# Loads of the later batches: each released by a score unit of its own, none by a program block; a new order of TensorE's units

## The chip, the cores and the metric

The kernel runs on one core of one Trainium2 chip. The metric is the time of one execution on the device in microseconds (us). The kernel before takes 405.16 us, the median of three runs (404.38 to 405.39).

## The reference

Inputs are q, k and v (8 batches, 12 heads, 448 positions, head size 64) and three weight matrices, all in float32. The kernel computes with bf16 operands, sums in f32 and writes f32.

```python
scores = q @ k.T / sqrt(64)                   # for each batch and head, 448 x 448
attn   = maximum(scores, 0) ** 2 / 448
x      = (attn @ v), heads side by side       # 3584 tokens x 768
g, val = x @ w_gate, x @ w_val                # 768 -> 1536 each
out    = (gelu(g) * val) @ w_out              # 1536 -> 768, f32, 3584 x 768
```

## The kernel before, in words

**Tiling.** A batch is 448 tokens. TensorE works as four quarters of 64 rows by 64 columns: nearly every matmul instruction is a 64x64 tile, the two column quarters of a row half get their matmuls one behind the other, and the two row halves (called 0 and 1) run beside each other, each with its own stream of work. The code keeps two lists for them, PE0 and PE1; a *unit* is a run of operations on row half 0 and, behind or beside it, the matching run on row half 1.

There are these kinds of unit:
- *score unit* (`add_scores`): 64 keys against 448 queries for two heads, or, for the last key block of a pair, for four heads with half the work each. There are 21 per batch, seven per group of four heads. A group of four heads of a batch is called a *third* here. Behind a score unit ScalarE does the ReLU (`emit_relu`, L695, out of PSUM tile `sp` into `rl`) and VectorE squares two units at a time (L709, `rl` into `attnT`).
- *value unit* (`add_values`): attention times v for two heads; the result goes to `xT`.
- *gate and value units* (`add_gate_value`) and *pair units* (`add_pair`): the two up-projections. The pair units do two 128-column blocks in seven half-size products, with sums of tokens (`ts`) and of weights (`ws`) made by VectorE ahead.
- *product units* (`add_product`): the down-projection, again as seven half-size products, with sums of `uT` (tiles `s`) and of the weights (`wt`). ScalarE copies some results into `osb` (L1205), VectorE adds the others (L1203), and SP stores finished tiles (L1221).

**What sets the order.** The string `LINE` gives the order of the gate, pair and product units: a single digit is a gate or value unit of that batch, `6A7` is product 7 of pair unit A of batch 6, `m4` is product 4 of token group m. The string `SHIFT` moves, for batches 2 to 7, the start and the end of the stretch over which a batch's score and value units are spread between them. A planner (`run_plan`) then takes units and operations one by one, keeps clocks for the engines and PSUM banks from costs written in the code, and so settles the order in which each engine's instructions are written into the program. On the chip each engine runs its own list in that order, and semaphores hold an instruction until what it needs is there.

**How a late third comes in.** Batches 0 and 1 are loaded up front and transposed on TensorE. The 18 thirds of batches 2 to 7 each take six loads on the POOL queue: q in two column parts, k in two column parts (`load_qk`, L407, 128 KB and 96 KB) and v in two halves (`load_v`, L426, 128 KB). When q and k are there, VectorE regroups them into `qkr` (L458), and SP issues two DMA transposes into `qkT` (L463). The score units then read `qkT`.

**What releases a late load.** Two things, both in the code around L1405 to L1418. First, `op.behind`: a load may not be issued before the ReLU of one named score unit of an earlier third has run (three thirds back for q and k, two for v). `PACE` says which of the seven units: `0, 0` for the two parts of q, `1, 2` for k, `4, 5` for v. Second, `op.gate`: the planner keeps a list of *marks*. TensorE's program comes in blocks of 256 instructions, and `Blocks` notes the matmul at which the next block is expected to be asked for. A load with a gate is put behind the latest mark (a semaphore on that matmul, added in `load`'s `paced`), and only if the loads since that mark fit into `BLOCK` = 7.1 us of the planner's time. The transposes on SP have such a gate too (`GATE_T` = 1.2).

```python
GATE_T, BLOCK = 1.2, 7.1
...
if not forced and max(traffic, t + 1.3) + op.gate > at + span:
    return None
```

Of the kernel before, what the change touches and what calls it, by code (L numbers as in the profile page):

```python
# [9 lines left out]


LINE = """
0 0 0 0 0 0 0 0 0 0 0 0 0 0 0 0 0 0 0 0 0 0 0 0 a1 1A1 1 1 1 2 a7 1 a2 1 1 1A6 1A2 1 a6 1 2 2A1 a5 1
1 2 1 1 1 2 1A7 2 1 a4 1 1A4 1A5 1 1 1A3 1 1 1 b1 b6 b7 a3 c1 c7 b5 2 b4 c6 2 2A7 2 2A6 2A5 b3 c5 2
c3 2A2 b2 2 2B1 2 2 c4 2B6 2A4 2B2 2B7 2B4 2A3 2B5 2 2 2 2 2B3 d1 3B1 d2 3B2 3B6 d7 3 3B7 3A1 c2 3A7
3 e1 3 3C1 3A6 d6 d5 3A2 3 3 3 3A5 3B4 e6 3A4 3C6 e7 3 3A3 d4 3C7 d3 e5 3B5 3 3C2 3 3C5 3B3 3 4C1
3C4 3C3 e2 3 3 4A1 4A2 4C6 e3 4C2 f1 f6 4A6 4 e4 4A7 f7 f2 f4 4C7 4D1 4B1 4 4C4 4B7 4 4B6 4 4D2 4A5
4B2 4B5 4 4 4C5 4D6 g1 4D7 g6 g7 4A4 4D5 g2 g4 5B1 5C1 4D4 4B4 4C3 5 f5 4 5B2 4A3 5C2 4B3 5 f3 4D3
5B6 5C6 g5 5C7 4 5A1 5C4 5B7 5 h1 5 5A6 5C5 h6 5A7 5D1 5 5A2 h2 h7 5 5B4 g3 5B5 5C3 5A5 5B3 5A4 6A1
5D7 5D2 h5 5D6 5D5 5D4 5 5A3 5D3 6A2 5 h3 i1 6B1 h4 6A7 i7 i2 6B2 6C1 i6 6B7 6C2 i5 6C6 6C7 j1 6D1  # L20
i4 6A6 6D6 6E1 6D7 j7 6A4 6F7 6D2 6A5 6E2 6B6 6A3 6D4 6E7 6F1 6B5 6F2 i3 6B4 6F6 6F5 6E6 6E5 6C5 6F4
j6 6E4 6C4 6F3 6C3 7E1 j2 6E3 6B3 7A1 7E2 6D5 7A2 j4 6D3 k1 7A7 k7 7E7 k2 k6 7E6 7B1 7C1 7B2 7B7 k5
l1 l7 7C7 7C2 7C6 j5 7D1 7A6 7E5 j3 l6 k4 7D6 7F1 7E4 7D2 7C5 7B6 7B4 7E3 7F6 7C4 l5 7A5 7F7 l2 7D7
7A4 7B5 7C3 7F5 k3 7F2 7B3 7D5 7D4 l3 7A3 7F4 7D3 7F3 m7 m1 l4 n1 m6 n7 n6 m5 n5 m3 n4 n3 m4 m2 n2
"""


# [3 lines left out]
"""  # L31


SHIFT = "-285.5 -165 37.25 3 -152 -99.5 -4.75 -19.75 18.25 -42.25 -369.75 2"


class Op:
# [223 lines left out]
def kernel(  # L261
# [30 lines left out]
    OGS = d_model // NG  # L292
    WOG = 3
    SB = 2
    PACE = 0, 0, 1, 2, 4, 5
    FB = 4
    FILL = 30.0
    EARLY = 2
# [60 lines left out]
    arrivals = {}  # L359
# [947 lines left out]
    for b in range(B):  # L1307
# [8 lines left out]
        if b >= EARLY:  # L1316
            lo, hi = lo + float(SHIFT.split()[2 * (b - 2)]), hi + float(SHIFT.split()[2 * (b - 2) + 1])
        if b >= EARLY:
# [89 lines left out]
    for n, (b, m) in enumerate(thirds):  # L1408
        if (b, m) > (2, 1):
            for i, op in enumerate(qk_loads[b, m]):  # L1410
                op.behind.append(relus[(*thirds[n - 3], PACE[i])])
        if (b, m) >= (2, 0):
            for i, op in enumerate(v_loads[b, m]):
                op.behind.append(relus[(*thirds[n - 2], PACE[4 + i])])
        for op in (*qk_loads[b, m], *v_loads[b, m]):
            op.deps += op.behind
            if b >= EARLY:
                op.gate = arrivals[op]  # L1418
    for new, old in zip(duos[RING_A:], duos):
        gone = [o_op[b, pr] for keys in old["of"] for b, pr, _ in keys]  # L1420
        for sq in new["sq"]:
# [46 lines left out]
```

## Time and profile before

| what | value |
|---|---|
| median of three runs | 405.16 us (404.38 to 405.39) |
| the profiled execution | 403.54 us, of it the span 401.5 us and 2.0 us around it |
| TensorE clock granted | 0.997 of full speed, mean |
| busy: TensorE matmul, weight load | 97%, 88% of the span |
| busy: VectorE, ScalarE, POOL | 77%, 65%, 24% |
| DMA bytes by POOL queue (q0) and by SP queue (q1) | 24.39 MB, 19.08 MB |

How to read it: busy times are shares of the span. A matmul's record has a modelled end, so TensorE can be counted busy while it waits; distances from one matmul's start to the next one's are exact, and the text uses those. A 64x64 matmul over 448 columns holds its quarter for 0.189 us (from start to start of matmuls on one quarter), over 224 columns for 0.096 us.

### The profile page before, as it was taken

To read this page: it belongs to the slowest core of one execution; us is meant where nothing else is said; L and a number is where in the kernel's file an instruction comes from. 1 tells how busy PE (TensorE), PEld (TensorE's weight loads), DVE (VectorE), ACT (ScalarE), POOL (GpSimd) and SP (SyncE) were. 2 spreads that over 40 slices of the span, in tenths; PEclk is the share of its full clock that TensorE was granted. 3 is DMA by queue.
4 is the path that set the end of the run, shared out by engine and by line. 5 is a ranking of instruction groups with operands and counts; after the bars stand their busy time and mean duration, and the time that the engine had idled before them with its cause. 6 is when DMAs were issued, how large, how long until landed. Compare 5 with 4: busy or idle time off the path is not lost.

```text
span 401.5 us, 22878 instructions
## 1 busy us (share of the span) xinstructions
PE 389.7 (97%) x10570; PEld 352.3 (88%) x10573; DVE 310.0 (77%) x522; ACT 259.6 (65%) x401; POOL 96.7 (24%) x156
## 2 busy tenths in 40 slices
PE   7999999999999999999999999999999999999994
PEld 3456788889997889988999999999999999999993
DVE  2785779877888679988898788568899988866671
ACT  4865772357686668868776787747787875525430
POOL 7567304423233233133331332103110000000000
PEclk9999999999999999999999999999999999999998
DMA  8999997998999987999499986736871301111115
GB/s 108 179 198 198 197 209 105 152 129 134 151 102 208 107 98 98 113 174 137 62 154 138 126 135 87 94 82 76 76 137 22 81 6 45 42 45 43 44 42 157
DMA packets 85086, 45.11 MB, mean 112 GB/s; under 512 B 45952, under 2 KB 81536, under 8 KB 84992
## 3 DMA queue, kind: packets, MB, share of 16 engines
q0 software_dynamic: 46944, 24.39, 49.6%
q1 hardware_dynamic: 37888, 19.08, 26.3%
q8 instruction: 82, 1.34, 1.4%
q10 hardware_dynamic: 160, 0.20, 0.2%
q14 instruction: 12, 0.10, 0.1%
HBM read 48.76 MB, written 11.01 MB: 149 GB/s over the span
## 4 chain that ended last, share of the span: by engine, by line
PE 97%; issue 1%; ACT 0%; DVE 0%
PE ff L349 84%; PE sp L349 9%; PE ff L548 1%; PE ff L1399 1%; PE sp L627 1%; PE ff L627 1%; PE ff L590 0%; ACT rl L695 0%; ACT qkT L598 0%; ACT osb L1205 0%; DVE warm L334 0%; DVE table L337 0%
## 5 line engine op out<-in xcount | busy, mean ns | idle before, releaser
L695 ACT ACTIVATE rl<-sp 128x896 bf16<-128x896 f32 x168 | 152.1, 919 | 55.2 <-PE sp L349 48.3
L349 PE MATMUL ff<-xT,wg 64*64 64x224 bf16 (+1 forms) x2304 | 180.5, 299 | 0.0
L349 PEld LDWEIGHTS <-wv 64*64 64x64 bf16 x2304 | 120.7, 107 | 8.2 <-issue 2.6
L349 PEld LDWEIGHTS <-wg 64*64 64x64 bf16 x2304 | 121.5, 107 | 6.1
L349 PE MATMUL ff<-xT,wv 64*64 64x448 bf16 x1056 | 120.6, 349 | 1.1 <-issue 0.9
L709 DVE TENSOR_TENSOR attnT<-rl 128x1792 bf16<-128x1792 bf16 (+1 forms) x98 | 92.3, 952 | 11.6 <-ACT rl L695 11.2
L349 PEld LDWEIGHTS <-ws 64*64 64x64 bf16 x1872 | 92.9, 107 | 1.9 <-issue 1.3
L349 PEld LDWEIGHTS <-s 64*64 64x64 bf16 x1344 | 82.5, 107 | 2.6
L349 PE MATMUL ff<-attnT,v 64*64 64x448 bf16 (+1 forms) x768 | 82.1, 326 | 0.3 <-issue 0.2
L349 PE MATMUL ff<-ts,ws 64*64 64x224 bf16 x1248 | 77.9, 256 | 1.4 <-issue 1.4
L349 PE MATMUL sp<-qkT 64*64 64x448 bf16 (+1 forms) x768 | 77.2, 331 | 1.5 <-issue 0.9
L349 PE MATMUL ff<-ts,wv 64*64 64x224 bf16 x1248 | 78.0, 256 | 0.0
L349 PE MATMUL ff<-wo,uT 64*64 64x384 bf16 x672 | 65.8, 322 | 0.0
L349 PEld LDWEIGHTS <-uT 64*64 64x64 bf16 x1008 | 63.1, 107 | 2.3 <-issue 0.9
L349 PE MATMUL ff<-wo,s 64*64 64x384 bf16 x672 | 64.4, 323 | 0.0
L947 DVE TENSOR_TENSOR part<-ff,part 128x448 f32<-128x448 f32 x78 | 47.4, 622 | 20.1 <-PE ff L349 13.9
L349 PE MATMUL ff<-wt,s 64*64 64x384 bf16 x672 | 62.7, 323 | 0.0
L426 POOL DMA_DIRECT2D v<-in_v_dram x48 | 29.6, 621 | 97.3 <-ACT rl L695 37.9
L943 ACT COPY part<-ff 128x448 f32<-128x448 f32 x78 | 41.2, 534 | 14.6 <-PE ff L349 12.8
L349 PEld LDWEIGHTS <-v 64*64 64x64 bf16 x768 | 45.6, 107 | 4.2 <-issue 1.8
L407 POOL DMA_DIRECT2D qk<-in_q_dram x43 | 27.2, 636 | 79.7 <-ACT rl L695 40.9
L349 PEld LDWEIGHTS <-qkT 64*64 64x64 bf16 x768 | 37.8, 106 | 8.3 <-issue 5.7
(51 smaller groups left out, 418.2 us busy)
## 6 DMA issues: line engine op xcount, KB each, us to landing
out_dram<-osb SPq DMA_DIRECT2D x54, 192.0 KB, 3.5
v<-in_v_dram POOLq DMA_DIRECT2D x48, 128.0 KB, 4.4
wg<-in_moe_w_gate_dram POOLq DMA_DIRECT2D x6, 384.0 KB, 10.1
wv<-in_moe_w_val_dram POOLq DMA_DIRECT2D x6, 384.0 KB, 11.2
wo<-in_moe_w_out_dram POOLq DMA_DIRECT2D x4, 576.0 KB, 15.4
qk<-in_q_dram POOLq DMA_DIRECT2D x18, 128.0 KB, 3.5
qk<-in_k_dram POOLq DMA_DIRECT2D x18, 128.0 KB, 4.9
qk<-in_q_dram POOLq DMA_DIRECT2D x18, 96.0 KB, 4.6
```

What stands on the lines that cost most here:

```text
L349: ins = nc.tensor.matmul(o, lhsT, rhs, start=start, stop=stop, skip_group_check=onto, tile_position=(P * row, P * col))
L407: return nc.gpsimd.dma_start(qk16[b, m][HALF[i], r0:r0 + h1 - h0, cols], src[b, h0:h1].rearrange("h (p c) d -> p h (c d)", c=SC)[:, :, cols])
L426: return nc.gpsimd.dma_start(v16[b, m][HALF[i], h0 % 4:h0 % 4 + h1 - h0, :, :], v[b, h0:h1].rearrange("h (p c) d -> p h c d", c=SC)[:, :, ...
L548: blocks.add(nc.tensor.matmul(t[:, :], warm[:, 0:128], warm[:, :], start=True, stop=True))
L627: blocks.add(nc.tensor.transpose(t[HALF[j], c, :], src[:, 2 * r + j, c, :], ident[:, :], tile_position=(0, P * j)))
L695: relu.ins = nc.scalar.activation(duo["rl"][:, u % 2, :, :], box[0][:, :, 0:S], AF.Relu).ins
L709: nc.vector.tensor_tensor(a[:, part], duo["rl"][:, part], duo["rl"][:, part], op=ALU.mult)
L943: rd.ins = nc.scalar.copy(st["t", name][:, :], box[0][:, 0:S]).ins
L947: rd.ins = nc.vector.tensor_tensor(t[:, :], box[0][:, 0:S], t[:, :], op=ALU.add).ins
L1399: blocks.add(nc.tensor.matmul(t[HALF[j], :], warm[:, HALF[j]], warm[:, :], start=True, stop=True, tile_position=(0, P * j)))
```

## The change

Three things change. `PACE` becomes `0, 1, 2, 3, 4, 5`, so the six loads of a third wait for six different score units. The late loads lose `op.gate`: they no longer wait for a mark, and the planner no longer counts whether they fit behind it; the transposes on SP keep theirs. `LINE` and `SHIFT` are written anew, which changes the order of the units; the program is the same for the first 1,650 of TensorE's 21,181 instructions (the first 52 us of the trace). The set of matmuls is the same (10,573).

```diff
 LINE = """
-0 0 0 0 0 0 0 0 0 0 0 0 0 0 0 0 0 0 0 0 0 0 0 0 a1 1A1 1 1 1 2 a7 1 a2 1 1 1A6 1A2 1 a6 1 2 2A1 a5 1
...
-7A4 7B5 7C3 7F5 k3 7F2 7B3 7D5 7D4 l3 7A3 7F4 7D3 7F3 m7 m1 l4 n1 m6 n7 n6 m5 n5 m3 n4 n3 m4 m2 n2
+0 0 0 0 0 0 0 0 0 0 0 0 0 0 0 0 0 0 0 0 0 0 0 0 1 1A1 1 2 1A6 2 2 1 1A7 1A2 1A5 2 a1 2 a2 2A1 1A4 1
...
+7F4 7D6 7D5 7D4 7D3 l2 7F5 7A4 7C5 7C3 7E3 7A3 l5 l4 7F3 m1 n1 m7 k3 l3 m2 m6 n6 m5 n7 n4 m3 n5 n2
+m4 n3
 """
...
-SHIFT = "-285.5 -165 37.25 3 -152 -99.5 -4.75 -19.75 18.25 -42.25 -369.75 2"
+SHIFT = "-183 -79.5 40.75 1.75 -343.75 -112 43.75 -179.5 27.25 -513.5 -447.25 0.25"
...
-    PACE = 0, 0, 1, 2, 4, 5
+    PACE = 0, 1, 2, 3, 4, 5
...
         for op in (*qk_loads[b, m], *v_loads[b, m]):
             op.deps += op.behind
-            if b >= EARLY:
-                op.gate = arrivals[op]
```

More of the change, by code (lines that the diff above doesn't have):

```diff
@@ L12 @@
 LINE = """
-0 0 0 0 0 0 0 0 0 0 0 0 0 0 0 0 0 0 0 0 0 0 0 0 a1 1A1 1 1 1 2 a7 1 a2 1 1 1A6 1A2 1 a6 1 2 2A1 a5 1
[L14 to L22, printed above, removed]
@@ L23 @@
-l1 l7 7C7 7C2 7C6 j5 7D1 7A6 7E5 j3 l6 k4 7D6 7F1 7E4 7D2 7C5 7B6 7B4 7E3 7F6 7C4 l5 7A5 7F7 l2 7D7
-7A4 7B5 7C3 7F5 k3 7F2 7B3 7D5 7D4 l3 7A3 7F4 7D3 7F3 m7 m1 l4 n1 m6 n7 n6 m5 n5 m3 n4 n3 m4 m2 n2
+0 0 0 0 0 0 0 0 0 0 0 0 0 0 0 0 0 0 0 0 0 0 0 0 1 1A1 1 2 1A6 2 2 1 1A7 1A2 1A5 2 a1 2 a2 2A1 1A4 1
+1 1 1A3 1 2 1 2A2 a6 1 2A7 a7 2 1 a5 1 1 2A6 2 2 1 1 1 1 a3 1 1 a4 1 1 b1 b7 c1 b2 b6 2A4 2 c6 b4 b5
+c7 c5 2B1 2B6 c4 2B2 c3 b3 2A5 2 c2 2B7 2B4 2B5 2A3 2 3A1 2 3A2 2 2B3 2 2 3A6 3A7 d7 d1 3B1 d2 4C1
@@ new lines @@
+3B2 3 3C1 3B7 3 d6 3 e1 d4 3C7 3 3C6 3 3B6 e7 3B4 e6 3A4 3A5 3 3 3 3C2 3 3B5 3 3 d5 3C4 3A3 3C5 d3
+4A1 4C2 3B3 3C3 e5 3 4A7 f1 f2 f6 e4 f7 4C7 4 e2 4C6 4A2 e3 g7 4B1 f5 4B6 4 4A6 4B2 g1 4B7 4 g2 4A5
+4C5 4A4 4B4 4B5 f4 4D7 4D1 4C4 4 5B1 5 4D6 4D5 4A3 4 g6 4 g5 4C3 4B3 f3 4 5 5B2 4D2 4D4 g3 4D3 5C1
+g4 5B6 5B7 5C2 5B5 5A1 4 5A6 5 5C7 5A7 5A2 5 5B4 5D1 h1 5A4 5D6 5D2 h6 5C6 h7 5 5D7 5D5 5A5 6A1 5B3
+5 5C5 5C4 5A3 5C3 5D4 6B1 5 5D3 5 6A2 6B2 h4 i1 i2 6B7 6A6 i7 h5 6A7 h2 6D1 6F7 6D7 h3 j1 6D6 6C1
@@ L25 @@
+6D2 i6 j7 6E1 j6 6C7 6C2 6E7 i5 i4 6C6 6B6 6A5 6A4 6E6 6A3 6F1 6B4 6B5 6C5 6D5 6D4 6F6 i3 6B3 6F5
+6C4 j5 6D3 6E2 6F2 6E5 6F4 6C3 6F3 6E4 6E3 7E7 j2 7E1 7B1 k1 k7 7E2 7A1 7B2 7B7 k2 7B6 7E6 j4 7C1 k6
+7A2 l7 7C7 7C6 7A7 7B4 7C2 l1 7B5 7B3 k5 7A6 7F1 j3 7D1 7E5 7F7 7F2 7A5 k4 7F6 7E4 l6 7D7 7C4 7D2
+7F4 7D6 7D5 7D4 7D3 l2 7F5 7A4 7C5 7C3 7E3 7A3 l5 l4 7F3 m1 n1 m7 k3 l3 m2 m6 n6 m5 n7 n4 m3 n5 n2
+m4 n3
 """
```

## The prediction, made before the changed kernel was run

> **What bounds the kernel now.** I read the page's busy times first, then the chain, then the waits of TensorE, and last the stretches of 40 us.
>
> ```profile
> span 401.5 us, 22878 instructions
> PE 389.7 (97%) x10570; PEld 352.3 (88%) x10573; DVE 310.0 (77%) x522; ACT 259.6 (65%) x401; POOL 96.7 (24%) x156
> ...
> q0 software_dynamic: 46944, 24.39, 49.6%
> q1 hardware_dynamic: 37888, 19.08, 26.3%
> q8 instruction: 82, 1.34, 1.4%
> ...
> PE 97%; issue 1%; ACT 0%; DVE 0%
> ```
>
> TensorE is the bound: the chain is its own work for 97%. The row q8 is its program being fetched by DMA: 82 packets for 10570 + 10573 instructions, so one packet of 16 KB per 256 instructions.
>
> ```profile
> 120.00:160.00 40.00, 38.19 (x979) 34.72 (x974) 31.66 (x50) 28.79 (x42) 12.49 (x20) 1.00 0.97 127
> 160.00:200.00 40.00, 38.90 (x1089) 36.54 (x1084) 34.05 (x56) 29.97 (x46) 11.48 (x19) 1.00 0.91 122
> 240.00:280.00 40.00, 40.00 (x1233) 39.39 (x1227) 29.20 (x49) 26.08 (x44) 6.73 (x11) 1.00 0.59 83
> ```
>
> The columns are length, then busy TensorE, weight load, VectorE, ScalarE, POOL, granted clock, DMA share and GB/s. TensorE has holes where the DMA share is above 0.9 and none where it is 0.59, at the same clock of 1.00. The waits of TensorE say what kind of hole it is:
>
> ```profile
> PE ff L349 <- issue: 2.5, 5, 0.9
> PE sp L349 <- issue: 0.9, 1, 0.9
> ```
>
> These are all of TensorE's waits between 100 and 330 us, and all are "issue": no semaphore is late. One of them up close, with the loads that POOL issued before it:
>
> ```profile
> 140.00 0.38 PE L349 MATMUL ff<-xT,wg 64*64 64x448 bf16 x2
> 141.33 0.28 PE L349 MATMUL ff<-ts,ws 64*64 64x224 bf16 x2 [0.95 <-issue]
> ```
>
> ```profile
> 134.75 1.22 POOL L407 DMA_DIRECT2D qk<-in_q_dram  x2 [5.31 <-ACT gel L1025]
> 135.96 0.63 POOL L407 DMA_DIRECT2D qk<-in_k_dram  x1
> 136.76 0.62 POOL L407 DMA_DIRECT2D qk<-in_k_dram  x1 [0.17 <-PE ff L349]
> ```
>
> In the trace's packets of q8 the fetch for this place starts at 138.51, takes 1.17 us, and TensorE goes on 1.65 us behind its end. The other holes look the same. From start to start, less the normal step, TensorE stands still at 128.7 (1.1 us), 140.0 (1.2), 177.0 (1.0), 187.0 (0.5), 192.4 (0.4), 215.7 (0.7) and around 317 to 322 (0.7), in sum 5.7 us with 0.1 of scatter; each ends 1.2 to 1.65 us after a q8 packet has landed. When a fetch meets little traffic, its packet starts before TensorE is 35 instructions into the next block; before these seven it is 77 to 131 instructions in. So the seven holes are fetches that stood behind other DMAs, and they are the stall time that a change of load timing can touch. Before five of the seven (128.7, 140.0, 177.0, 192.4 and 215.7, in sum 4.4 us) the four q and k loads of one third had been issued within 2.0 to 3.8 us, as in the rows above; before the hole at 187.0 stand v loads, a transpose and stores, before the last one stores alone.
>
> **The change part by part.** The profiled execution is 403.54 us: span 401.5 and 2.0 around it. The median is 1.6 above it. I work the sum as a difference on the profiled one and put it on the median, 405.16.
>
> *The new order on TensorE, taken by itself.* The matmuls are the same. I walked both lists with the steps that the trace shows (0.189 us per 448 columns, 0.096 per 224, each row half by itself). The old order walked so follows the trace to 0.1 us between the seven holes, so it can carry a difference. Where one row half has nothing next in the list while the other works, time is lost: 0.7 us in the old order behind 45 us, 1.6 us in the new one (the largest are 0.2 to 0.4 us on one half, eight of them, around 72, 162, 250 to 262 and 299 us). Cost: +0.9 us. It is on the path, since nothing covers TensorE.
>
> *The release of the loads.* 108 late loads, issued between 65 and 299 us, so one per 2.2 us in the mean; 28 of the 107 distances are under 0.8 us, which is POOL working through a bunch (one issue is 0.62 us). With six different units per third, and POOL's program no longer holding a load for a mark, the q and k loads of a third come about one score unit apart, some 2.2 us each, so the four take some 6.5 us where the bunches took 2.0 to 3.8. This thins the traffic ahead of a fetch. Against it: nothing now keeps a load from arriving just ahead of one. The trace does not show late loads without marks. Its bounds: the least is that all seven holes go, −5.7 us. The most, from the nearest rows: the up-front weight loads have no marks either, and fetches under them start 3.5 to 4.4 us behind the point where an undisturbed one starts 0.6 to 1.7 us behind it; were five more of the late fetches hit as the seven are (0.8 us each), it would be +4.1 us. I take a value between: of the 4.4 us that follow bunches of four loads half stays (2.2), and the two others stay (1.2). Left 3.4 instead of 5.7 us: −2.3 us. I choose the lower half because the bunch stands before five of seven holes and the bytes do not change; new holes are a rival below.
>
> *Waits for data.* A q or k load now hangs on a unit up to one place later, 2.2 us. Behind it stand the regrouping (L458), two transposes on SP's queue, and the third's first score. In the trace the second transpose lands 1.4 us ahead of the first score at 82.8, 4.6 at 95.4, 1.8 at 108.1 and 7.7 us or more ahead for all fifteen thirds after that. The last q or k load is issued 15.7 us ahead of the first score at the first late third and 25.9 us or more at the others. So I cost the later load at nothing; the cover is this lead. In the three early thirds the transposes, which keep their marks, decide, not the loads; with 1.4 to 1.8 us of cover a transpose that comes one block mark later (3 to 6 us) would cost 1.5 to 4 us. POOL's queue holds nothing but loads, so nobody else waits behind a held load; on SP's queue stores (L1221) stand behind a held transpose, and the four `osb` buffers hold back ScalarE's copies, for which the trace shows no wait by TensorE.
>
> *The end.* The last products are m4 and n3 instead of m2 and n2. The last read is a ScalarE copy (L1205, 479 ns in the mean) in place of a VectorE add (L1203, 556 ns), and the same four stores follow. I take 0; it may be 0.1 us either way.
>
> Sum: +0.9 − 2.3 + 0 + 0 = −1.4 us, so 402.1 on the profiled execution's own time and 403.8 on the median.
>
> One rule of the Trainium skill speaks against this reading. "Runtime: NRT & Kernel Launch", in the section on instruction fetch mechanics, says that a program is streamed in 16 KiB blocks of 256 instructions and that crossing a block is mostly hidden. The trace agrees with the block (82 packets) and not with the hiding (5.7 us in seven places). By that rule the fifth rival would hold. A second, from "DMA: Bandwidth & Descriptors", section "Queues, rings and completion order", says that a DMA engine goes round its queues packet by packet, so that a fetch would wait for one packet per queue and not for whole loads. The trace shows waits of 3 to 5 us behind sustained traffic where single data packets last 0.03 to 0.18 us, so I do not count on it.
>
> **The rivals.**
> - *More fetches are hit (slower).* Without marks a load arrives ahead of a fetch by chance, at any of the 50 fetches between 65 and 300 us, with a DMA share over 0.9 up to 240 us. For: the early unmarked loads delay every fetch under them. Against: they are 384 KB each and back to back. It decides from the point where the holes' sum passes 4.8 us (5.7 − 0.9); at nine holes of 0.8 us, 7.6 us, the time is 405.16 + 0.9 + 1.9 = 408.0.
> - *As many holes as now, in other places (no change).* Sum 4 to 6 us: 404.4 to 406.4, all inside 0.3% of the median; at 5.0 us, 405.4. For: traffic and fetches are as many, and the transposes and stores are still there. Against: the bunches go.
> - *Nearly all holes go (faster by more).* Only the two without a bunch of four stay, 1.2, or less: 405.16 + 0.9 − 4.5 = 401.6, and 401.1 with the store hole alone. For: the bunches are what five of seven have in common. Against: a transpose and a store or two also make up the traffic.
> - *A third's transposes come late (slower).* The early thirds have 1.4 to 1.8 us of cover; two of them late by one mark beyond that, 2 us each, give 403.8 + 4 = 407.8.
> - *The holes have nothing to do with the loads (no change).* Then they stay, at 5.7 us in sum, and the order alone counts: 405.16 + 0.9 = 406.1. For: the hole at 317 to 322 us has no load near it. Against: from 240 to 280 us, at a DMA share of 0.59, there is no hole at the same rate of instructions. The page on the runtime, named above, would give this time too.
>
> **How the numbers follow.** 0.3% of 405 is 1.2 us; that is about what a measurement of this kernel can tell from no change. Chances: the forecast's own case (holes of 2.5 to 4 us) 0.33, nearly all gone 0.12, as many as now 0.22, not the loads 0.05, more hit 0.21, late transposes 0.07. The first case reaches from 402.8 to 404.3, and 404.0 is the bound of 0.3%, so some 0.06 of it falls inside; of "more hit" nothing falls inside by its definition, and 0.04 of "as many" goes over to slower for scatter. That gives faster 0.33 − 0.06 + 0.12 = 0.39, same 0.06 + 0.18 + 0.05 = 0.29, slower 0.21 + 0.07 + 0.04 = 0.32. The range: below it reaches to 400.8, the store hole alone with 0.3 of scatter; above to 408.4, nine holes with 0.4. The forecast's own range is 402.6 to 404.6.
>
> **What the changed profile would show.** The holes are again "issue" waits of TensorE and each ends some 1.5 us behind a q8 packet; there are four or five, in sum some 3.4 us. POOL's waits for late loads name the ReLU (L695 before, one line on after) and no longer matmuls, and fewer than ten distances are under 0.8 us. The walk of the new order leaves 0.9 us more. I am wrong if TensorE waits for a semaphore of VectorE or of a transpose, or if the holes' sum is over 5 us.

## The result and the profile after

| kernel | median | lowest to highest | executions |
|---|---|---|---|
| before | 405.39 us | 402.29 to 412.97 | 19 |
| after | 402.40 us | 400.90 to 404.77 | 19 |

The ratio of after to before is 0.9926, with a 95% interval of 0.9907 to 0.9945: the change makes the kernel about 3.0 us (0.7%) faster. The forecast was 403.8, so the direction was right and the gain twice what I had worked out (−3.0 in place of −1.4). 402.40 lies inside the whole range (400.8 to 408.4) and just below the forecast's own (402.6 to 404.6). Ratios here leave out executions that lie more than 1.5% above the fastest of the same kernel, which trims a kernel whose time scatters widely, so medians of all executions stand beside them.

The profiled execution of after took 402.81 us (span 400.7), that of before 403.54 (span 401.5). Their difference is only 0.7, and this is the first thing to learn from: the profiled execution of before lies 1.9 us under the median of before in the table, that of after 0.4 above its own. Lines of the page of after:

```profile
span 400.7 us, 22892 instructions
PE 391.1 (98%) x10573; PEld 357.8 (89%) x10573; DVE 309.4 (77%) x522; ACT 259.0 (65%) x401; POOL 97.2 (24%) x156
...
q0 software_dynamic: 46944, 24.39, 50.0%
q1 hardware_dynamic: 37888, 19.08, 27.7%
q8 instruction: 82, 1.34, 1.4%
...
PE 95%; DMA 2%; POOL 1%; issue 1%; ACT 0%; POOLq 0%
```

TensorE is the bound as before, with the same matmuls, the same bytes and the same 82 packets of its program. Two stretches of 40 us of after:

```profile
120.00:160.00 40.00, 39.63 (x1046) 37.91 (x1040) 30.75 (x49) 29.09 (x43) 11.30 (x18) 1.00 1.03 138
160.00:200.00 40.00, 40.00 (x1153) 38.99 (x1147) 36.18 (x60) 30.17 (x47) 11.64 (x19) 1.00 0.85 114
```

These two, where before lost most (TensorE busy for 38.19 and 38.90), are now at 39.63 and 40.00. The DMA share is higher in the first (1.03 against 0.97) and lower in the second (0.85 against 0.91). All waits of TensorE between 100 and 330 us in after:

```profile
PE ff L350 <- issue: 1.0, 3, 0.4
```

They are again "issue", as the prediction said, and no semaphore is late. The largest hole that is left lies in this piece of after's timeline:

```profile
225.49 0.32 PE L350 MATMUL ff<-wt,s 64*64 64x384 bf16 x1
226.20 0.35 PE L350 MATMUL ff<-wt,s 64*64 64x384 bf16 x1 [0.39 <-issue]
```

Ahead of it POOL had issued nothing since 217 us, and SP these stores:

```profile
221.46 4.26 SPq L1222 DMA_DIRECT2D out_dram<-osb  x4
```

The packet of q8 for this place ran from 223.92 to 224.84; TensorE went on at 226.20, 1.36 us behind its end. Only two of the four stores had been issued when the packet started (at 221.46 and 221.97, landing at 224.45 and 226.29); the other two followed at 224.60 and 225.14. And what POOL's late loads waited for between 65 and 300 us, first in before, then in after:

```profile
POOL qk L407 <- ACT rl L695: 52.5, 29, 5.6
POOL v L426 <- ACT rl L695: 37.9, 18, 3.9
POOL qk L407 <- PE ff L349: 26.0, 8, 18.3
POOL v L426 <- PE ff L349: 11.3, 5, 4.5
```

```profile
POOL qk L408 <- ACT rl L696: 89.7, 55, 8.0
POOL v L427 <- ACT rl L696: 30.5, 24, 3.9
POOL qk L408 <- PE ff L350: 4.1, 3, 1.5
POOL v L427 <- PE ff L350: 0.9, 1, 0.9
```

In before, 13 of the waits (37 us) end on a matmul, as a wait for a mark does, and 47 on a ReLU; in after, where no load waits for a mark, four still end on a matmul (5 us) and 79 on a ReLU. Distances between late loads under 0.8 us fall from 28 to 7. The four q and k loads of a third are issued within 5.1 us in the median, 3.4 in before.

**How the sum of the holes is measured.** I walk TensorE's list with the traced steps, as in the prediction, and set the walked starts against the traced ones: the distance grows only where TensorE stands still. What it grows by behind 46 us is the sum of the holes. The time of an execution is then the walk, plus the start (the distance at 46 us), plus the holes, plus 7.7 to 8.0 us for the rest. A second profiled execution of each kernel was taken as well (old_again and new_again, the kernels unchanged):

| profiled execution | time | walk | start | holes, sum |
|---|---|---|---|---|
| before | 403.54 | 382.91 | 6.69 | 5.95 |
| before, again (old_again) | 409.02 | 382.91 | 5.86 | 12.28 |
| after | 402.81 | 383.82 | 7.41 | 3.68 |
| after, again (new_again) | 402.39 | 383.82 | 5.55 | 5.32 |

Where the holes lie says what they are. Count the instructions that a trace holds for TensorE (matmuls, weight loads and some 33 of its sequencer) in order of their start: each of the 37 holes in these four profiles that are over 0.3 us from start to start stands behind the 190th or 191st instruction of a round of 256 (193rd or 194th in the first profile of after, whose trace holds three more matmuls). With one packet per 256 instructions, that is one crossing of a block of the program each time. In these four profiles all 44 holes end 1.2 to 1.7 us after a q8 packet has landed.

The holes of before are not the same each time. In its second profile they are twice as long in sum. Five of before's seven crossings have a hole again (those at 128.7, 140.0, 177.0, 192.4 and 215.7 us), and eleven holes of over 0.3 us lie at other crossings. The largest of old_again is the one that before has at 215.7; from start to start it grows from 0.76 to 2.08 us. First before, then old_again:

```profile
215.67 0.35 PE L349 MATMUL ff<-attnT,v 64*64 64x448 bf16 x1
216.43 0.25 PE L349 MATMUL ff<-ts,ws 64*64 64x224 bf16 x1 [0.41 <-issue]
```

```profile
216.21 0.26 PE L349 MATMUL ff<-ts,ws 64*64 64x224 bf16 x1
218.29 0.25 PE L349 MATMUL ff<-ts,ws 64*64 64x224 bf16 x1 [1.76 <-issue]
```

Ahead of it stand the four q and k loads of one third, issued within 4.1 us, and two stores and a transpose from SP, in old_again:

```profile
209.36 1.22 POOL L407 DMA_DIRECT2D qk<-in_q_dram  x2 [2.62 <-ACT rl L695]
211.13 0.76 POOL L407 DMA_DIRECT2D qk<-in_k_dram  x1 [0.55 <-ACT rl L695]
212.81 0.61 POOL L407 DMA_DIRECT2D qk<-in_k_dram  x1 [0.92 <-ACT rl L695]
```

```profile
211.27 1.11 SPq L1221 DMA_DIRECT2D out_dram<-osb  x2
212.49 1.75 SPq L463 DMA_TRANSPOSE qkT<-qkr  x1
```

In before the same seven stand there, each 0.5 us earlier, as TensorE is. Yet the last k load and the transpose take 5.8 and 6.3 us to land there and 6.9 and 7.3 in old_again, and the fetch's packet starts at 213.98 in before and at 215.65 in old_again. So the same group in the same place costs 1.3 us more in one execution than in the other. Why the DMAs of the group are slower in one of them, the traces do not show.

Not every hole stands behind other DMAs. Two of after's and three of new_again's (between 367 and 375 us, 0.25 to 0.55 us from start to start) follow a fetch with no other packet in flight on the core from 3 us before its start to its end. What delays these is not shown.

### The profile page after: what moved, and what is told of

The parts are those of the page before. It is cut to its first block, busy times and chain, and to the rows that moved or that the text cites. A ratio compares the mean times of both kernels' runs of the same rounds, so it can differ in the third digit from the quotient of the medians.

```text
span 400.7 us, 22892 instructions
## 1 busy us (share of the span) xinstructions
PE 391.1 (98%) x10573; PEld 357.8 (89%) x10573; DVE 309.4 (77%) x522; ACT 259.0 (65%) x401; POOL 97.2 (24%) x156
## 3 DMA queue, kind: packets, MB, share of 16 engines
q0 software_dynamic: 46944, 24.39, 50.0%
## 4 chain that ended last, share of the span: by engine, by line
PE 95%; DMA 2%; POOL 1%; issue 1%; ACT 0%; POOLq 0%
PE ff L350 85%; PE sp L350 8%; DMA qk<-in_k_dram 2%; PE ff L549 1%; PE sp L628 1%; POOL qk L408 1%; PE ff L628 1%; ACT rl L696 0%; ACT osb L1206 0%; POOL ident masks.py:199 0%; POOL ident masks.py:197 0%; POOLq L1451 0%
## 5 line engine op out<-in xcount | busy, mean ns | idle before, releaser
L350 PE MATMUL ff<-xT,wg 64*64 64x224 bf16 (+1 forms) x2304 | 183.4, 299 | 0.2 <-issue 0.2
L350 PEld LDWEIGHTS <-wv 64*64 64x64 bf16 x2304 | 128.4, 107 | 5.0 <-issue 0.6
L350 PEld LDWEIGHTS <-wg 64*64 64x64 bf16 x2304 | 124.6, 107 | 5.1 <-issue 0.6
L350 PEld LDWEIGHTS <-s 64*64 64x64 bf16 x1344 | 81.6, 107 | 3.8 <-issue 1.8
L350 PE MATMUL ff<-attnT,v 64*64 64x448 bf16 (+1 forms) x768 | 80.5, 326 | 0.1
L350 PE MATMUL ff<-ts,wv 64*64 64x224 bf16 x1248 | 79.3, 256 | 0.0
L350 PE MATMUL ff<-wo,uT 64*64 64x384 bf16 x672 | 61.8, 322 | 0.3 <-issue 0.3
```

Source lines behind the costliest of these rows:

```text
L350: ins = nc.tensor.matmul(o, lhsT, rhs, start=start, stop=stop, skip_group_check=onto, tile_position=(P * row, P * col))
```

## The experiments

Before them I had four theories on what brings the gain: the q and k loads of a third no longer come in pairs (spacing); the marks themselves made bunches, so their removal brings it; the new order brings it; or the marks protect the fetches, and the change gains in spite of their loss. The kernels named old_ start from before, those named new_ from after. Where only a wait of a load or of a store is changed, and where the stores are shortened, every engine's list of instructions is that of the kernel it starts from. They ran in three groups, each with before beside it; the median of before was 406.77, 407.51 and 406.08 in them, so each kernel is compared with the before of its own group.

### Marks and spacing in the new order, and marks in the old one

*new_mark: after, and each late load waits for the latest mark too.*

```diff
-            if op.mark is not None:
-                tc.add_manual_dep(ins.ins, op.mark.ins.name, SYNC, reason="pace")
+            if op.late and blocks.marks:
+                tc.add_manual_dep(ins.ins, blocks.marks[-1][1].ins.name, SYNC, reason="pace")
...
+            op.late = b >= EARLY
```

This mark is the latest one at the load's place in the list. The count of what fits behind a mark, which before has in its planner, is not put back.

> The changed kernel with its order, in which each late load also waits for the latest mark before it; all engines' lists as in the changed kernel. Theory A (spacing): 402 to 403.5, since the six units per third still hold. Theory B (marks make the bunches): 404.5 to 406. Theory C (order alone): 402.4, no change. Theory D (marks protect): 401 to 402.

Measured: 402.95 (6 executions; before 406.77), ratio 0.9887 [0.9844, 0.9930]. That is the gain of after, no more and no less within the intervals. With the loads spaced and the order new, marks change nothing that can be measured here.

*new_pairs: after, but the q and k loads wait for units 0, 0, 1, 2 as before (the planner's own view, and so all lists, unchanged; no marks).*

```diff
-            for d in op.behind:
+            for d in op.waited or op.behind:
...
+                op.waited = [relus[(*thirds[n - 3], (0, 0, 1, 2)[i])]]
```

> The changed kernel with its order, in which the q and k loads wait on the chip for the score units 0, 0, 1, 2 of the old rule instead of 0, 1, 2, 3; no marks; all engines' lists as in the changed kernel. Theory A (spacing): the two parts of q come 0.6 us apart again, holes grow by 1 to 2 us, 403.5 to 405. Theory B (marks): 402.4, no change. Theory C (order alone): 402.4, no change.

Measured: 408.81 (12 executions), ratio 1.0014 [0.9980, 1.0048]. The whole gain is gone, and more than the theory of spacing expected. Against after, only the moment at which three of a third's four q and k loads may start has changed, by one unit, with the same five lists of instructions. Each less its own before, the two lie 5.0 us apart by the medians (+2.0 and −3.0) and some 3.6 by the ratios. (New_mark, in the same group as new_pairs, is 5.9 us faster, but it has marks as well as spacing.) The holes' sum in its profile is 11.58 us (16 places). The main rows of TensorE's waits in new_pairs behind 46 us, the largest hole in the timeline, and what was issued ahead of it on POOL and on SP:

```profile
PE ff L350 <- issue: 2.8, 8, 0.9
PE ff L350 <- DVE attnT L711: 2.3, 1, 2.3
PE sp L350 <- DMA qkT<-qkr: 0.3, 1, 0.3
```

```profile
153.26 0.60 PE L350 MATMUL ff<-xT,wg 64*64 64x448 bf16 x12
156.17 0.38 PE L350 MATMUL ff<-xT,wv 64*64 64x448 bf16 x2 [2.31 <-DVE attnT L711]
```

```profile
148.22 1.22 POOL L409 DMA_DIRECT2D qk<-in_q_dram  x2 [3.34 <-ACT rl L697]
150.79 0.61 POOL L409 DMA_DIRECT2D qk<-in_k_dram  x1 [1.35 <-ACT rl L697]
152.47 0.61 POOL L409 DMA_DIRECT2D qk<-in_k_dram  x1 [1.06 <-ACT rl L697]
```

```profile
148.05 1.11 SPq L1223 DMA_DIRECT2D out_dram<-osb  x2
149.25 2.11 SPq L465 DMA_TRANSPOSE qkT<-qkr  x1
```

It is much the group of old_again once more: two q loads back to back, two k loads, two stores and a transpose within 5 us. The last k load, issued at 152.47, lands at 159.26. The fetch started at 153.41 and landed at 154.37; TensorE went on 1.80 us later. The row names VectorE's `attnT` as the releaser, and that had ended at 155.85. The hole lies at a crossing (behind the 191st instruction of its round), so a fetch is part of it; whether its last part is the wait for `attnT` is not shown. One small hole, 0.46 us at 107.5, is a score that waits for its transpose (the row with `qkT`), and it lies at no crossing; the other 14 end 1.3 to 1.6 us after a q8 packet.

*new_mark_pairs: pairs and marks under the new order.* It has the edits of the two kernels above together.

> The changed kernel with its order and both old rules of release put back on the chip (marks, and score units 0, 0, 1, 2). Theory A and theory B: 404.5 to 406.5, the gain is gone, and 0.9 us of the order's cost stays. Theory C (order alone): 402 to 403.

Measured: 403.20 (11 executions), ratio 0.9908 [0.9871, 0.9944]; holes 3.9 us in its profile (7 places, one of them again the transpose at 107.5). The gain is kept: in the new order marks alone keep what spacing keeps, 5.6 us against new_pairs. It also says that the new order brings the whole gain with pairs and marks, nearly as the loads had them in before. The loads are no less bunched than there: 32 distances are under 0.8 us, 28 in before. So a bunch as such does not make the holes; where it falls in the order does, as far as these runs tell.

*old_nomark: before, the loads no longer wait for marks; the list as planned with them.*

```diff
-            if op.mark is not None:
-                tc.add_manual_dep(ins.ins, op.mark.ins.name, SYNC, reason="pace")
```

> The kernel before with its old order, in which the late loads no longer wait for a mark on the chip; the planner still counts the marks, so all five engines' lists are those of before. The walk of TensorE's list is unchanged. Theory A (spacing: the two parts of q on one score unit make bunches, and bunches delay the fetches): the pairs stay, so little is won, 404.5 to 406. Theory B (the marks make the bunches, since POOL holds several loads behind one matmul and then lets them go together): 402 to 403.5, as fast as the changed kernel less the 0.9 us of its order. Theory C (the new order alone brings the gain, by where it puts stores and transposes): 405 to 406, no change. Theory D (marks do protect the fetches): 407 or more.

Measured: 407.34 (12 executions; before 406.77), ratio 1.0027 [0.9992, 1.0062]. In the old order and with pairs, marks make no difference that can be measured; the theory that they made the bunches falls.

### Spacing in the old order

*old_mark_spread: before, marks kept, q and k loads on units 0, 1, 2, 3. old_spread: the same without marks.*

```diff
...
+            if op.waited is not None:
+                held_back.append((ins, op.waited))
-            for d in op.behind:
+            for d in op.behind if op.waited is None else ():
...
+                op.waited = relus[(*thirds[n - 3], i)]
...
+    for ins, relu in held_back:
+        tc.add_manual_dep(ins.ins, relu.ins.name, SYNC, reason="pace")
```

> The kernel before with its old order and marks, q and k loads behind score units 0, 1, 2, 3 on the chip. Theory spacing: 403 to 405. Theory order alone: 405.5 to 407, no change.

> The kernel before with its old order and with the changed kernel's rule of release put in on the chip alone: no marks for loads, q and k loads behind score units 0, 1, 2, 3 of the earlier third. All engines' lists as before. If the new release rule works by itself (spacing wins in any order): 402 to 404. If it only works together with the new order: 405 to 408, and the holes' sum stays at 6 to 9 us.

Measured: with marks 404.22, ratio 0.9930 [0.9899, 0.9962]; without marks 406.03, ratio 0.9940 [0.9899, 0.9982] (12 executions each; before 407.51; one of old_spread stands far off at 678.87, at a granted clock of 0.559, and one of before at 821.14). So spacing alone is worth 1.5 to 3.3 us in the old order by the medians. For old_mark_spread this is clear; the interval of old_spread rests on seven of its twelve executions, so its gain is likely and no more. The profiled executions of these two were among their slower ones (406.5 and 408.24, holes 8.6 and 10.0 us), so their sums do not show the gain. They do show where spacing acts. From 120 to 160 us TensorE is busy for the whole 40.00 in both, where before has 38.19 and old_again 37.98, at about the same DMA share. In old_spread:

```profile
120.00:160.00 40.00, 40.00 (x1054) 37.20 (x1049) 33.98 (x53) 30.73 (x45) 12.92 (x21) 1.00 0.96 134
```

From 160 to 240 us they lose more than before does, in the largest hole 2.66 and 1.84 us from start to start, at 180 us.

The eight cases together, as median minus the median of before in the same group:

| order | late loads wait for marks | units of q and k | kernel | median less before's | ratio |
|---|---|---|---|---|---|
| old | yes | 0, 0, 1, 2 | before | 0 | 1 |
| old | no | 0, 0, 1, 2 | old_nomark | +0.6 | 1.0027 |
| old | yes | 0, 1, 2, 3 | old_mark_spread | −3.3 | 0.9930 |
| old | no | 0, 1, 2, 3 | old_spread | −1.5 | 0.9940 |
| new | yes | 0, 0, 1, 2 | new_mark_pairs | −3.6 | 0.9908 |
| new | yes | 0, 1, 2, 3 | new_mark | −3.8 | 0.9887 |
| new | no | 0, 0, 1, 2 | new_pairs | +2.0 | 1.0014 |
| new | no | 0, 1, 2, 3 | after | −3.0 | 0.9926 |

All four kernels with spaced loads gain (old_spread the least surely); of the four with pairs only one does. The parts do not add: there is one gain of some 3 us to be had, and spacing gets it in either order, marks only in the new one.

### The stores

*old_nostore and new_nostore: all stores but those of the last token group write 16 of 768 columns, so most of the output is left out.*

```diff
+            if not final:
+                part = slice(0, 16)
             engine.dma_start(rows[c, :, part], osb[t][HALF[j], part])
```

> The kernel before, in which each store of a finished tile, but for those of the last token group, writes 16 columns instead of 768: the output is left incomplete, some 10 MB of stores are gone from the DMA queues, and nothing else is changed on TensorE, VectorE, ScalarE and POOL. If the holes are fetches behind other DMAs, of stores too: the hole at 317 to 322 us goes, those at 128.7 and 177 (with six and four stores ahead) shrink, and the time is 2 to 4 us less, 402 to 404. If the holes have nothing to do with DMA traffic: no change, 405 to 407. If loads and transposes alone make them: the hole at 317 to 322 goes and nothing else, 405 to 406.

> The changed kernel with its stores cut to 16 of 768 columns but for the last token group (output incomplete), as done before to the old order. In the old order that took some 6 us. If the new order's gain is that its stores stand better to the fetches: little is left to take, 0.5 to 2 us, 400.5 to 402, and the new order is then no faster than the old one without stores (400.9). If the new order gains by loads and transposes: the stores still cost 4 to 6 us, 396.5 to 398.5.

Measured: 400.92 against 407.51 in the old order (ratio 0.9846 [0.9785, 0.9907]), 398.68 against before's 406.08 in the new one (0.9807 [0.9751, 0.9864]), 4 executions each. In the old order this is more than the 2 to 4 us expected. The stores cost 6.6 us there; in the new order the difference to after is 7.4 − 3.0 = 4.4 us. With intervals of some ±2.5 us on each, the two are not told apart. One stretch of each, old_nostore first:

```profile
120.00:160.00 40.00, 40.00 (x1052) 37.12 (x1048) 33.98 (x54) 30.91 (x45) 13.73 (x22) 1.00 0.90 106
```

```profile
120.00:160.00 40.00, 40.00 (x1061) 38.91 (x1056) 31.34 (x50) 29.66 (x44) 12.29 (x20) 1.00 0.82 99
```

Both profiles of before have holes in this stretch (two and five, 1.1 to 1.2 us the largest); old_nostore has none, although its late loads still come in bunches (28 distances under 0.8 us, as in before). The hole around 317 to 322, which had no load near it, is gone too. The holes' sums are 4.07 and 1.77 us. So in this execution a bunch of loads alone is not enough in this stretch: it takes loads and stores together. Five holes at 162 to 213 us stay in old_nostore (0.2 to 0.9 us), with no large store left to blame, and three at 370 to 378 us, two of them with no other packet in flight around the fetch.

*new_store_next: after, with the stores of token groups 0 to 11 waiting for the next mark.*

```diff
...
+            if gr < 12:
+                held_back.append((ins, len(blocks.marks)))
...
+    for ins, n in held_back:
+        tc.add_manual_dep(ins.ins, blocks.marks[n][1].ins.name, SYNC, reason="pace")
```

> The changed kernel, in which each store of a finished tile, but for those of the last two token groups, also waits for the next mark, that is for the matmul at which the next block of TensorE's program is asked for; all engines' lists are those of the changed kernel. If stores ahead of a fetch make holes and stores just behind its request do not: the holes' sum falls from 3.7 to 2 or less and the time is 400 to 401.5. If the held stores only make bunches of another kind, or hold up the transposes behind them on SP: 402.5 to 405.

Measured: 406.60 (12 executions, 401.10 to 409.11; before 406.08), ratio 0.9955 [0.9910, 1.0000]; holes 7.68 us in its profile, two of them 1.3 and 1.7 us. By the medians most or all of the gain is lost, more than either case expected, though the executions scatter widely. Moving the stores behind a mark gains nothing; that they then meet other traffic is a guess.

### The order without its plan

*old_nogate: before, the late loads without their gate already in the planner; `LINE`, `SHIFT` and `PACE` as before.*

```diff
-            if b >= EARLY:
-                op.gate = arrivals[op]
```

> The kernel before with the gate taken from the late loads in the planner, and nothing else: old LINE, SHIFT and PACE. The planner then makes another order of all lists; the walk of TensorE's list comes to 390.4 us instead of 382.9. If the walk is right: 7 us slower than before, 411 to 415. If the holes in a row half are filled on the chip: 405 to 409.

Measured: 416.0 (4 executions; before 406.08), ratio 1.0242 [1.0171, 1.0314]. The planner then writes another list; its walk is 390.39 us, 7.5 more than before's, and the holes are 10.3 us. The largest of TensorE's waits in it for a semaphore:

```profile
PE sp L349 <- DMA qkT<-qkr: 2.4, 1, 2.4
```

It is a score that waits for a transpose, the very thing that the rival of the late transposes describes, here at 110 us. Under the old `LINE` the gate could not be taken out of the planner without a loss; another order had to come with it.

## Why the prediction was right, and where it was off

*What bounds the kernel, and what the holes are.* Right for the most part. The holes are late fetches of TensorE's program, each at a crossing of a block, and other DMAs make most of them: same lists and same bytes, and a wait moved by one unit costs 3.6 to 5.0 us (new_pairs against after). This also throws out the rival in which the holes have nothing to do with the loads. A few fetches are late with no other DMA in flight, which the prediction did not see. (Its 77 to 131 instructions into the next block are counted from the first instruction of the trace; from the crossings themselves they are 143 to 197.) The Trainium skill ("Runtime: NRT & Kernel Launch", section "Instruction fetch mechanics") says that the crossing of a block is mostly hidden. Here that holds for most crossings and not for all: of the 82 fetches of an execution 8 to 18 are followed by a hole, 3.7 to 12.3 us in sum.

*The new order by itself, +0.9 us.* Right as a walk (382.91 to 383.82). But it was put down as the order's only effect, and here the prediction had the wrong sign: new_mark_pairs, the new order with pairs and marks, gains 3.6 us. The order also decides which loads, stores and fetches fall together. An order's traffic can't be left out of its price.

*The release of the loads, −2.3 us.* That spacing the loads shortens the holes was right: it gains in the old order, and without it and without marks the new order gains nothing. Its worth depends on the order, though. In the old order the new release rules bring 1.5 us (old_spread, not surely); in the new order, where marks and pairs already have the gain, they bring none (−3.6 to −3.0). So the prediction's split into an order that costs and a release that gains is not what the runs show, and that its sum came out on the right side owes something to luck. The spacing was also overrated: I had the four loads of a third over 6.5 us, and they take 5.1.

The sum of holes after was near: forecast 3.4, measured 3.68 and 5.32. The sum of before from which I subtracted was too small. I took the 5.7 us of one profiled execution for the kernel's, although its time lay 1.6 us under the median, and carried the difference along as a mere offset. That the offset was mostly holes is likely and not shown. With 12.28 us in the second profile the mean of the two is 9.1, against 4.5 for after. As an estimate from these means, release and order together take 4.6 us off the holes, and −4.6 + 0.9 = −3.7, near the −3.0 measured; two profiles of each kernel are few, and old_again ran in a group where before's median was 2.1 us higher. I also ascribed two holes to other traffic and five to loads, as if each had one cause; the shortened stores show one stretch where loads and stores make them together.

*Marks.* I let the case in which unmarked loads hit more fetches have 0.21. After shows nothing of it, new_mark is not faster than after, and old_nomark not slower than before by a measured amount. But new_pairs shows that marks can matter: without spacing, taking them away costs 5.6 us in the new order (408.81 against 403.20).

*Waits for data, 0, and the end, 0.* Right: no wait of TensorE for a semaphore in after, and the remainder outside walk, start and holes is 8.0 us in the first profile of before and 7.9 in that of after.

*The signs named in advance.* The holes are "issue" waits: right. Four or five of them: there are eight, each smaller (0.2 to 0.7 us). Fewer than ten short distances: seven. ReLU instead of matmuls: nearly, four waits on matmuls are left. A sum of over 5 us was named as a sign of being wrong: the first profile (3.68) keeps under it, the second (5.32) does not, although its time is 402.39. The argument that there is no hole at a DMA share of 0.59 does not stand as I made it, as the same stretch of old_again shows:

```profile
240.00:280.00 40.00, 37.92 (x1140) 36.49 (x1139) 27.21 (x45) 23.82 (x40) 6.06 (x10) 1.00 0.62 78
```

At a share of 0.62, TensorE has holes at 245.1 us (1.17 from start to start) and at 259.1 (0.77). The mean share of a stretch does not tell whether a fetch is hit; the few microseconds ahead of it tell more, though not all, as the same group at 215.7 us shows.

*What stays open.* Why marks protect the fetches in the new order and not in the old one is not settled. Nor is it settled how much of the new order's part lies with its stores, why the same traffic delays a fetch more in one execution than in another, and what delays the fetches that meet no other DMA. No kernel with its whole output was clearly faster than after; new_mark, new_mark_pairs and old_mark_spread gain as much within the scatter (3.8, 3.6 and 3.3 us).

## What to carry to other kernels

Where a long unrolled program bounds the kernel and its bound engine shows "issue" holes, the program's own fetch may be competing with the kernel's DMAs: see whether the holes lie at one place in the count of 256 instructions, spread loads that belong together over several units of work, and look at loads, stores and transposes in the few microseconds ahead of each fetch, not at mean shares. If the profiled execution lies away from the median, ask what the difference consists of before working a sum on it; a second profile of the unchanged kernel would have shown here that the stalls to be saved can be twice what the first one said. Changing the release of DMAs and the order together needs all the combinations to tell them apart, since they can stand in for one another.

## What the runs showed of the hardware

- The same program loses 5.95 us in holes in one execution and 12.28 in another; the time from start to end follows it (403.54 and 409.02).
- In four profiles all 44 holes end 1.2 to 1.7 us after a packet of q8 has landed, whatever the size of the hole, and the 37 over 0.3 us from start to start all lie at one place in the count of 256 instructions.
- A fetch can be late with nothing else in flight: in new_again three fetches from 365 to 373 us, with no other packet on the core from 3 us before, are followed by holes of 0.53, 0.55 and 0.35 us from start to start.
- The start before 46 us differs by up to 1.9 us between executions of the same kernel (7.41 and 5.55 in after), which no term of the prediction held.
- Under such traffic a load itself is slow: in new_pairs the k load issued at 152.47 us, behind two stores, three loads and a transpose, had its last byte at 159.26, 6.8 us later. The median from issue to landing of a third's first k load is 5.4 us there and 4.4 in after, for the same bytes. The Trainium skill says in "DMA: Bandwidth & Descriptors", section "Queues, rings and completion order", that a DMA engine goes round its queues packet by packet, with several descriptors to a packet. By that a fetch would slip in between these loads. The prediction set the trace's single packets of 0.03 to 0.18 us against this rule; they are 519 bytes in the mean on q0 (24.39 MB in 46944), and nothing here shows that they are packets in the Trainium skill's sense, so the rule is neither borne out nor refuted. No run shows what the fetch waits for inside an engine, only that it lands late and that the kernel is faster where the loads are spaced.
